# Weight and token parts of a split-precision feed-forward kernel: made by ScalarE and accumulating DMAs instead of VectorE and GpSimd, and six more units computed from parts

## The chip, the cores and the metric

The kernel runs on one core of a Trainium2 chip. The metric is the device time of one execution in microseconds. The kernel before takes 273.64 us (median of three runs, 273.51 to 273.93). One execution was also recorded by the hardware profiler; that one took 273.72 us, of which the profile shows a span of 272.0 us. All times inside the kernel are microseconds from the start of that span.

## The reference

Two blocks follow each other. The first is a linear attention with sketched quadratic features; the second a gated feed-forward block on its output.

```
phi(x)  = outer(S1 x, S2 x)                 # r = 8, so 64 features, per token and head
q_p, k_p = phi(q), phi(k)                   # q, k, v: batch 4, heads 4, 1088 tokens, 32 wide
kv  = sum over s of k_p[s] v[s]             # 64 x 32 per head
z   = sum over s of k_p[s]
x   = (q_p kv) / (q_p z + 1e-6)             # -> 4352 tokens x 128
g   = x @ w_gate ;  val = x @ w_val         # 128 -> 1536
out = (g * sigmoid(g) * val) @ w_out        # 1536 -> 128
```

The inputs come as 64-bit floating-point numbers and are handled as pairs of 32-bit words.

## The kernel before

**Tiles.** Tokens stand in the columns of `xT` (128 features x 4352 tokens) and are worked on in blocks: the first batch's 1088 tokens as blocks 0, 1 and 2 (384, 320 and 384 columns), the rest in blocks of 480. The 1536 hidden features are 12 chunks `j` of 128. A *unit* (i, j) is block i against chunk j: two products into PSUM (gate and value), Silu on ScalarE, the product of both on VectorE into a slot of `hbuf`, `extra`, `soon` or `late`. `down()` multiplies a finished unit by chunk j of `w_out` and sums over j in one PSUM bank for each block.

**Plain units and units of parts.** `unit()` multiplies plain 32-bit floats (line 1043); each of its two products shows as two MATMUL records. The other kind replaces a product by three faster ones in the format fp32r: weight and token are each split into a high part, a low part and a difference part (`w1`, `wb`, `wd` and `x1`, `x0`, `xd`). `start_unit()` (line 1007) makes `wd` times `xd` for gate and value, and ScalarE then scales those sums in PSUM (line 1010). `finish_unit()` adds `w1` times `x1` and `wb` times `x0` for both (lines 1019 and 1020), then Silu (1022) and the product (1027). Both multiply six times in all.

**Where parts come from.** Before they are split, the weights arrive as 64-bit words in pieces, and `narrow()` turns each piece to 32 bits in four steps: VectorE (265, 266), ScalarE (270, 271), VectorE (273, 279), and a multiply on GpSimd (288) that writes the weight. `cut_weights(w, c)` then splits the three chunks 3c to 3c+2 of `w_gate` or `w_val` in four steps, each 128 x 384: `w1` on ScalarE (859), the remainder on GpSimd or VectorE (862), `wb` on ScalarE (864), `wd` on VectorE or GpSimd (867, 871). `cut_tokens(i)` splits a block of tokens, `cut_down()` the chunks 1 to 11 of `w_out`.

**Order.** The schedule is written out by hand: each engine runs its instructions strictly in the order in which the program issues them, and SyncE (SP), ScalarE and GpSimd issue DMAs from the same in-order queues. The stretch that matters here has four stages:

- A list `seq` of 24 units of the first batch, here numbered 0 to 23: (0,3) to (0,5), (2,0) to (2,2), (1,3) to (1,5), (2,3) to (2,5), (0,6) to (0,8), (1,6) to (1,8), (0,9) to (0,11), (1,9) to (1,11). All 24 are plain. From unit 17 on each is followed by a `down()`. Between them `parts[z]` holds the narrowing steps of the last weight pieces and of `w_out`, and `attentions()` gives steps of the next batch's attention through `parts_of()`.
- A loop of ND = 13 `down()` calls with attention steps between: after the eighth come `key_values` (393), `key_products` (359) and `value_sums` (718), which needs the sums that GpSimd makes in `feature_sums` (552); after the eleventh come `query_sketches` (347). The twelfth pass begins with `start_unit(2, 6)`, the first unit of parts.
- Units (2, 6) to (2, 11), of parts, each with a `down()`, then further `down()` calls.
- The main loop over the blocks of 480, all of parts, with the second batch's attention and onward between.

`steps_at` says after which unit or pass of a loop a step of `cut_weights` or `cut_tokens` is issued; the names are `g0` to `g3` and `v0` to `v3` for the four thirds of `w_gate` and `w_val`, `x` for the tokens of block 2. `accum_op` DMAs (issued on GpSimd, which add what they bring to what is there) are already used in the main loop, for the difference part of the hidden values (988), after a plain copy issued on SP (978).

Of the kernel before, what the change touches and what calls it, by code (L numbers as in the profile page):

```python
# [19 lines left out]
def kernel(  # L20
# [599 lines left out]
    def attentions():  # L620
# [4 lines left out]
        kp = pair("keys")  # L625
        for i, c in enumerate(kpieces):
            key_products(kp[:, i, :], *c)
        ka = apool.tile([P, NC * H, R], FP32, tag="kas", name="kas")

        def sketch(ps, i):  # L630
            c0, c1 = kpieces[i]
            return ps[:, i, 0 : 64 * (c1 - c0)].rearrange("p (x t r) -> p x t r", t=2, r=R)

        for i, (c0, c1) in enumerate(kpieces):
            nc.scalar.copy(ka[:, H * c0 : H * c1, :], sketch(kp, i)[:, :, 0, :])
        yield from turn_queries(1)
        phk = apool.tile([P, NC, H, R, R], FP32, tag="phk", name="phk")
        for n, (i, c0, c1) in enumerate(((0, 0, 3), (0, 3, 5), (1, 5, 7), (1, 7, 9))):
            first = H * (c0 - kpieces[i][0])
            kb = sketch(kp, i)[:, first : first + H * (c1 - c0), 1, :]  # L640
            key_features(phk, (ka[:, H * c0 : H * c1, :], kb), c0, c1)
            if n == 0:
                zs, sums = feature_sums(phk)
            else:
                sums.pop(0)()
            if n == 3:
                let_go("keys")
            if n % 3 != 1:
                yield
# [194 lines left out]

    def home(w, c):


# [7 lines left out]
    def cut_weights(w, c, low, engine):  # L855

        w1, wb, wd = w_parts[id(w), c] = home(w, c)
        src = w[:, 3 * c : 3 * c + 3, :]
        nc.scalar.activation(out=w1, in_=src, func=AF.Copy, scale=CUT)
        yield  # L860
        low = low[0]
        engine.tensor_tensor(out=low, in0=src, in1=whole(w1), op=ALU.subtract)
        yield
        nc.scalar.activation(out=wb, in_=low, func=AF.Copy, scale=BETA)
        yield
        if engine is nc.vector:
            nc.vector.scalar_tensor_tensor(
                out=wd, in0=low, scalar=-BETA, in1=whole(w1), op0=ALU.mult, op1=ALU.add
            )
        else:  # L870
            engine.tensor_tensor(out=wd, in0=whole(w1), in1=whole(wb), op=ALU.subtract)

    def cut_tokens(i, engine=nc.gpsimd, soon=False):
# [7 lines left out]
        nc.scalar.activation(x1[:, 0:n], x, AF.Copy, scale=CUT)  # L881

        def low():
            engine.tensor_tensor(
                out=x0[:, 0:n], in0=x, in1=whole(x1[:, 0:n]), op=ALU.subtract
            )

        def difference():
            nc.vector.scalar_tensor_tensor(
                out=xd[:, 0:n], in0=whole(x1[:, 0:n]), scalar=WHOLE, in1=x,  # L890
                op0=ALU.mult, op1=ALU.subtract,
# [33 lines left out]
    def cut_down():  # L925

        n = len(FINE)
        parts = const.tile([P, 3, n, D], F32R, tag="room", name="dparts", bufs=1)
        w1, wb, wd = (parts[:, k] for k in range(3))
        down_parts.update(w1=w1, wb=wb, wd=wd)  # L930

        def high(c):
            nc.scalar.activation(w1[:, c], wo[:, FINE[0] :][:, c], AF.Copy, scale=CUT)

        def left(c):
            nc.gpsimd.tensor_tensor(
                out=wb[:, c], in0=whole(w1[:, c]), in1=wo[:, FINE[0] :][:, c], op=ALU.subtract
            )

        def differ(c):  # L940
            nc.vector.scalar_tensor_tensor(
                out=wd[:, c], in0=whole(wb[:, c]), scalar=BETA, in1=whole(w1[:, c]),
                op0=ALU.mult, op1=ALU.add,
            )

        a, b, c = slice(0, 3), slice(3, 6), slice(6, n)
        high(a)
        yield
        high(b)
        yield  # L950
        high(c)
        add_to(behind, 2, lambda: left(a))
        add_to(behind, 2, lambda: left(b))
        add_to(behind, 5, lambda: differ(a))
        add_to(behind, 6, lambda: differ(b))
        add_to(behind, 2, lambda: left(c))
        add_to(behind, 21, lambda: differ(c))
        yield

# [35 lines left out]
    room = const.tile([P, 10, BW], FP32, tag="room", name="room", bufs=1)  # L995
# [39 lines left out]
    def unit(i, j, late=False, between=(None, None), apart=False):  # L1035
# [10 lines left out]
        sg = room[:, len(lates) + caught[0], :] if late else fpool.tile([P, WB], FP32, tag="sg", name="sg", bufs=5)  # L1046
# [25 lines left out]
    def down(y=None):  # L1072
# [11 lines left out]
        if j in mine:  # L1084
            w1, wb, wd = [down_parts[x][:, FINE.index(j), :] for x in ("w1", "wb", "wd")]
# [22 lines left out]
    def copy_out(y, i, n):  # L1108
# [4 lines left out]
        copy = lambda: nc.scalar.activation(x, p, AF.Copy, scale=-BETA * WHOLE)  # L1113
# [200 lines left out]
    def free(c):  # L1314
        return [room[:, c, :].rearrange("p (c f) -> p c f", f=P)]

# [12 lines left out]

    lows = {}  # L1330
    cuts = {"x": cut_tokens(2, nc.vector, soon=True)}
    for c in (2, 3, 0, 1):
        cuts["g%d" % c] = cut_weights(wg, c, free(8 + c % 2), nc.vector if c else nc.gpsimd)
        lows["v%d" % c] = free(6 + c % 2)
        cuts["v%d" % c] = cut_weights(wv, c, lows["v%d" % c], nc.vector if c == 1 else nc.gpsimd)
# [11 lines left out]
    steps_at = {20: ("v2",), 21: ("v3", "v2", "v3"), 22: ("g2",), 23: ("g3",)}  # L1347
    for z, (i, j) in enumerate(seq):
# [3 lines left out]
        unit(i, j)  # L1352
# [6 lines left out]
        if z >= 17:  # L1359
            next_down()  # L1360
            parts_of(1)
# [132 lines left out]
```

## Time and profile before

| | |
|---|---|
| time, median of three | 273.64 us |
| time of the profiled execution | 273.72 us |
| its span | 272.0 us |
| TensorE (PE) busy | 265.8 us, 98% |
| VectorE (DVE) busy | 223.3 us, 82% |
| ScalarE (ACT) busy | 199.6 us, 73% |
| GpSimd (POOL) busy | 87.5 us, 32% |
| chain that ended last | PE 92% of the span |

Busy shares are means over the whole span. Matmuls are pipelined: a record's duration includes its latency, and the pace is read from the distance between the starts of two neighbours. A row of the timeline holds start, duration, engine, line, operation and tiles, `x2` for two merged instructions; the brackets behind it hold the idle time of the engine before the row, and what ended it. "To landing" is counted from the start of a DMA's issue to its semaphore.

### The profile page before, as it was taken

The page shows a single profiled execution, that of the slowest core. Times are in us where ns is not written, and L with a number is a line of the kernel's source. Part 1 is how long each engine was busy: PE and PEld are TensorE (multiplying, and loading weights), DVE is VectorE, ACT ScalarE, POOL GpSimd, SP SyncE. Part 2 cuts the span into 40 slices and gives each one's busy share as a digit, 9 for nine tenths or more (in the row PEclk, how much of TensorE's full clock was granted, in tenths as well). Part 3 has the DMA queues.
Part 4 walks back from the last instruction along what each step waited for, and adds up shares of the span by engine and source line. Part 5 has one row for each costly group of instructions (what it writes and reads, how often), then busy time and mean ns, then how long its engine had stood idle before and what let it go on. Part 6 is the DMA issues. An engine that isn't in the chain of part 4 may idle for free.

```text
span 272.0 us, 6028 instructions
## 1 busy us (share of the span) xinstructions
PE 265.8 (98%) x2212; PEld 204.0 (75%) x2212; DVE 223.3 (82%) x429; ACT 199.6 (73%) x357; POOL 87.5 (32%) x110
## 2 busy tenths in 40 slices
PE   8899999999999999999999999999999999999994
PEld 7645566666785687886677878867888888889994
DVE  3997988989788798987767889768968996998881
ACT  3468666362686789787579998869989888888870
POOL 3313422249431494470042342223224213222000
PEclk9999999999999999999999999999999999999999
DMA  6573197131331047811137869754476566647221
GB/s 194 172 212 95 49 260 215 40 127 29 94 90 27 1 120 189 180 49 39 39 88 178 177 140 187 180 108 123 86 160 155 118 136 147 146 103 153 39 36 29
DMA packets 36509, 32.01 MB, mean 118 GB/s; under 512 B 20992, under 2 KB 34560, under 8 KB 36480
## 3 DMA queue, kind: packets, MB, share of 16 engines
q1 hardware_dynamic: 30064, 22.13, 28.3%
q0 software_dynamic: 5184, 8.85, 19.0%
q10 hardware_dynamic: 1232, 0.66, 0.9%
q8 instruction: 17, 0.28, 0.4%
q14 instruction: 12, 0.10, 0.1%
HBM read 11.41 MB, written 2.23 MB: 50 GB/s over the span
## 4 chain that ended last, share of the span: by engine, by line
PE 92%; DVE 3%; DMA 2%; ACT 1%; issue 0%; SPq 0%; ACTq 0%
PE PS L1095 14%; PE PS L1019 14%; PE PS L1007 14%; PE PS L1020 14%; PE PS L1043 12%; PE PS L1087 5%; PE PS L1089 5%; PE PS L1090 5%; PE PS L359 2%; PE PS L792 2%; PE PS L347 2%; PE PS L393 2%; DMA kld<-in_k_dram 2%; PE PS L1133 1%; PE PS L502 1%; PE PS L450 1%
## 5 line engine op out<-in xcount | busy, mean ns | idle before, releaser
L1010 ACT ACTIVATE PS<-PS 128x960 f32<-128x960 f32 (+1 forms) x90 | 83.4, 926 | 22.1 <-PE PS L1007 20.6
L1027 DVE SCALAR_TENSOR_TENSOR hbuf<-PS,sg 128x480 f32<-128x480 f32 (+1 forms) x81 | 51.8, 639 | 21.2 <-ACT sg L1022 20.1
L1022 ACT ACTIVATE sg<-PS 128x480 f32<-128x480 f32 (+1 forms) x90 | 49.6, 552 | 2.2 <-PE PS L1020 1.9
L1007 PE MATMUL PS<-xd,wd 128*128 128x480 f32 (+1 forms) x90 | 33.6, 373 | 0.0
L1020 PE MATMUL PS<-x,wb 128*128 128x480 f32 (+1 forms) x90 | 33.5, 372 | 0.0
L1019 PE MATMUL PS<-x,w 128*128 128x480 f32 (+1 forms) x90 | 33.3, 370 | 0.0
L1095 PE MATMUL PS<-hbuf,wo 128*128 128x480 f32 (+3 forms) x80 | 33.0, 505 | 0.0
L1007 PE MATMUL PS<-xd,graw 128*128 128x480 f32 (+1 forms) x69 | 32.6, 472 | 0.0
L1020 PE MATMUL PS<-x,graw 128*128 128x480 f32 (+1 forms) x69 | 25.5, 370 | 0.0
L1043 PE MATMUL PS<-xT,wg 128*128 128x384 f32 (+1 forms) x60 | 23.5, 474 | 0.1
L1043 PE MATMUL PS<-xT,wv 128*128 128x384 f32 (+1 forms) x60 | 23.1, 467 | 0.3 <-DVE wv L288 0.3
L1007 PEld LDWEIGHTS PS<-xd,wd 128*128 128x128 f32 x90 | 16.9, 188 | 6.3 <-issue 2.3
L1047 ACT ACTIVATE sg<-PS 128x384 f32<-128x384 f32 (+1 forms) x24 | 11.2, 468 | 13.2 <-PE PS L1043 12.4
L1019 PEld LDWEIGHTS PS<-x,w 128*128 128x128 f32 x90 | 16.9, 187 | 2.2
L1020 PEld LDWEIGHTS PS<-x,wb 128*128 128x128 f32 x90 | 16.9, 188 | 2.1
L1019 PE MATMUL PS<-x,graw 128*128 128x480 f32 (+1 forms) x48 | 18.0, 376 | 0.0
L1095 PEld LDWEIGHTS PS<-hbuf,wo 128*128 128x128 f32 x80 | 14.8, 189 | 3.8 <-issue 0.4
L1007 PEld LDWEIGHTS PS<-xd,graw 128*128 128x128 f32 x69 | 13.0, 188 | 5.3 <-ACT PS L1010 1.9
L1043 PEld LDWEIGHTS PS<-xT,wv 128*128 128x128 f32 x60 | 11.2, 190 | 7.4 <-DVE hbuf L1058 0.8
L1043 PEld LDWEIGHTS PS<-xT,wg 128*128 128x128 f32 x60 | 10.9, 190 | 7.7 <-issue 1.1
L1019 PE MATMUL PS<-x,gphq 128*128 128x480 f32 (+1 forms) x42 | 16.1, 384 | 0.1
L1020 PEld LDWEIGHTS PS<-x,graw 128*128 128x128 f32 x69 | 13.0, 188 | 1.3
(287 smaller groups left out, 589.5 us busy)
## 6 DMA issues: line engine op xcount, KB each, us to landing
kld<-in_k_dram SPq DMA_DIRECT2D x4, 544.0 KB, 4.2
qld<-in_q_dram SPq DMA_DIRECT2D x3, 544.0 KB, 5.3
raw<-in_moe_w_out_dram SPq DMA_DIRECT2D x4, 384.0 KB, 4.6
hwv<-hwv POOLq DMA_DIRECT2D x6, 240.0 KB, 3.5
hextra<-hextra POOLq DMA_DIRECT2D x6, 240.0 KB, 3.5
vld<-in_v_dram SPq DMA_DIRECT2D x9, 144.0 KB, 5.2
hwv<-hwg SPq DMA_DIRECT2D x5, 240.0 KB, 3.0
hkld<-hqld SPq DMA_DIRECT2D x5, 240.0 KB, 2.5
```

What stands on the lines that cost most here:

```text
L1007: nc.tensor.matmul(ps[:, k], w_parts[id(w), j // 3][2][:, j % 3, :], xd, start=True, stop=True)
L1010: nc.scalar.activation(ps, ps, AF.Copy, scale=-1.0 / WHOLE)
L1019: nc.tensor.matmul(ps[:, k], w1, x1, start=False, stop=False, skip_group_check=True)
L1020: nc.tensor.matmul(ps[:, k], wb, x0, start=False, stop=True, skip_group_check=True)
L1022: nc.scalar.activation(sg, ps[:, 0], AF.Silu, scale=WHOLE)
L1027: nc.vector.scalar_tensor_tensor(out=hj[:, 0:n], in0=ps[:, 1], scalar=WHOLE, in1=sg, op0=ALU.mult, op1=ALU.mult)
L1043: nc.tensor.matmul(o[:, 0:n], w[:, j, :], xT[:, t0 : t0 + n], start=True, stop=True)
L1047: nc.scalar.activation(sg[:, 0:n], g[:, 0:n], AF.Silu)
L1087: nc.tensor.matmul(acc[i][:, 0:n], wd, hd, **sides)
L1089: nc.tensor.matmul(p, w1, h1, start=(j == mine[0]), stop=False)
L1090: nc.tensor.matmul(p, wb, h0, start=False, stop=(j == mine[-1]))
L1095: nc.tensor.matmul(acc[i][:, 0:n], wo[:, j, :], hidden[i, j][:, 0:n], **sides)
```

## The change

`cut_weights` no longer uses VectorE or GpSimd arithmetic. ScalarE makes `w1` with the sign turned; an accumulating DMA issued on GpSimd adds it to the weight in place, which leaves the remainder there, and a DMA issued on SP copies `w1` to `wd`; ScalarE makes `wb` from the remainder; a second accumulating DMA adds `wb` to `wd`. Each of the two accumulating DMAs and the copy moves 128 x 384 floats (192 KB). `cut_tokens` gets the same form of `x0` for blocks 0, 1 and 2 (copy on SP, accumulation on GpSimd), and `cut_down` for its low part, now in four groups of up to three chunks.

The last three chunks (c = 3) of both weights are split right behind their narrowing, during units 10 to 15, and blocks 0 and 1 of the tokens are split as well, so that units 18 to 23 become units of parts. The third with c = 2 and the tokens of block 2 follow in the ND loop; c = 0 and c = 1 later. The keys' sketches of the first `attentions()` step are copied whole from PSUM by ScalarE (both factors, not one). Buffers move: the parts of c = 3 and of `w_out` take over the spots of `room`, now six single tiles, and a new tile `more`.

```diff
-    def cut_weights(w, c, low, engine):
+    def cut_weights(w, c):
         w1, wb, wd = w_parts[id(w), c] = home(w, c)
         src = w[:, 3 * c : 3 * c + 3, :]
-        nc.scalar.activation(out=w1, in_=src, func=AF.Copy, scale=CUT)
+        nc.scalar.activation(out=w1, in_=src, func=AF.Copy, scale=-CUT)
         yield
-        low = low[0]
-        engine.tensor_tensor(out=low, in0=src, in1=whole(w1), op=ALU.subtract)
+        nc.gpsimd.dma_start(out=src, in_=whole(w1), accum_op=ALU.add)
+        nc.sync.dma_start(out=whole(wd), in_=whole(w1))
         yield
-        nc.scalar.activation(out=wb, in_=low, func=AF.Copy, scale=BETA)
+        nc.scalar.activation(out=wb, in_=src, func=AF.Copy, scale=BETA)
         yield
-        if engine is nc.vector:
...
+        nc.gpsimd.dma_start(out=wd, in_=wb, accum_op=ALU.add)
...
     def cut_tokens(i, engine=nc.gpsimd, soon=False):
...
+        if engine is None:
+            nc.sync.dma_start(out=whole(x0[:, 0:n]), in_=x)
         def low():
+            if engine is None:
+                nc.gpsimd.dma_start(out=x0[:, 0:n], in_=x1[:, 0:n], accum_op=ALU.add)
+                return
...
     def cut_down():
...
+            def left(w1=w1, wb=wb):
+                nc.gpsimd.dma_start(out=wb, in_=w1, accum_op=ALU.add)
...
+            nc.scalar.activation(w1, src, AF.Copy, scale=-CUT)
+            nc.sync.dma_start(out=whole(wb), in_=src)
+            add_to(behind, 2, left)
+            add_to(behind, (5, 6, 21, 22)[g], differ)
...
-    steps_at = {20: ("v2",), 21: ("v3", "v2", "v3"), 22: ("g2",), 23: ("g3",)}
+    FIRST = 18
+    steps_at = {
+        10: ("g3",), 11: ("v3", "g3"), 12: ("v3", "x0"), 13: ("g3",), 14: ("v3", "g3", "x0"),
+        15: ("v3", "x1"), 17: ("x1",),
+    }
     for z, (i, j) in enumerate(seq):
...
-        unit(i, j)
+        if z < FIRST:
+            unit(i, j)
+        else:
+            if z + 1 < len(seq):
+                start_unit(*seq[z + 1])
+            finish_unit(i, j)
         for p in parts.get(z, ()):
             part(*p)
...
         if z >= 17:
             next_down()
             parts_of(1)
+        if z + 1 == FIRST:
+            start_unit(*seq[FIRST])
...
     steps_at = {
-        0: ("g2", "v2", "v3"), 1: ("g2",), 2: ("g2", "g3"), 3: ("g3", "v2"), 4: ("g3", "v3"), 5: ("g2",),
-        7: ("x",), 8: ("x", "g3", "v0"), 9: ("g0",),
+        0: ("v2",), 1: ("g2", "v2"), 2: ("g2",), 3: ("x2", "v2"), 4: ("g2",), 5: ("x2", "v2"), 6: ("g2",),
+        8: ("v0",), 9: ("g0", "v0"), 10: ("g0",), 12: ("v0", "g0"),
     }
     ND = 13
...
     steps_at = {
-        7: ("v0", "g0"), 9: ("v0", "g0"), 10: ("v0", "g0"), 11: ("v1", "g1", "v1", "g1"),
+        6: ("v0",), 7: ("g0", "v1"), 8: ("g1", "v1"), 9: ("g1",), 10: ("v1",), 11: ("g1",),
     }
```

The resulting order on GpSimd from unit 10 on is: the narrowing multiply of the last piece of `w_val`; the first accumulations of g3 and v3; the multiply of `w_out` piece 0; the second accumulation of g3; that of the tokens x0; the second accumulation of v3; the multiply of `w_out` piece 1; tokens x1; the multiplies of pieces 2 and 3; the four operations of `feature_sums`; the first accumulations of v2 and g2; the tokens x2; the second accumulations of v2 and g2; then those of c = 0 and c = 1. On ScalarE, `wb` of g3 stands ahead of unit 14's Silu, and `wb` of v3 ahead of unit 15's.

## The prediction

> **What bounds the kernel now.** I read the page's busy shares and the chain that ended last first.
>
> ```profile
> PE 265.8 (98%) x2212; PEld 204.0 (75%) x2212; DVE 223.3 (82%) x429; ACT 199.6 (73%) x357; POOL 87.5 (32%) x110
> ...
> PE 92%; DVE 3%; DMA 2%; ACT 1%; issue 0%; SPq 0%; ACTq 0%
> ```
>
> TensorE is the chain. A busy PE need not be at its peak, so I then read TensorE's own timeline, start to start.
>
> ```profile
> 45.19 0.70 PE L1043 MATMUL PS<-xT,wg 128*128 128x320 f32 x2
> ...
> 48.42 0.81 PE L1095 MATMUL PS<-hbuf,wo 128*128 128x384 f32 x2
> 49.06 0.81 PE L1043 MATMUL PS<-xT,wg 128*128 128x384 f32 x2
> 49.71 0.81 PE L1043 MATMUL PS<-xT,wv 128*128 128x384 f32 x2
> 50.35 0.81 PE L1095 MATMUL PS<-hbuf,wo 128*128 128x384 f32 x2
> ...
> 72.39 0.44 PE L1007 MATMUL PS<-xd,graw 128*128 128x384 f32 x1
> ...
> 74.27 0.34 PE L1019 MATMUL PS<-x,graw 128*128 128x384 f32 x1
> 74.44 0.34 PE L1020 MATMUL PS<-x,graw 128*128 128x384 f32 x1
> ```
>
> Plain products of 384 columns follow each other by 0.645 us, products of parts by 0.174. From about 30 us to 240 us nearly every distance is at its pace: the matmul work itself sets the end, and nothing downstream has slack to take back a TensorE stall. A microsecond of product saved is a microsecond gained, a microsecond waited is one lost. VectorE and GpSimd work taken away gains nothing by itself.
>
> **Part 1: six units of parts (gain).** A plain unit of 384 columns takes 2 x 0.645 = 1.29 us, one of parts 6 x 0.174 = 1.05: 0.245 saved, three times. At 320 columns the plain unit takes 1.075 (45.19 to 46.26), and six parts scaled from 0.174 at 384 and 0.217 at 480 take 6 x 0.146 = 0.88: 0.195 saved, three times. Sum: **-1.3 us**. That is all that TensorE can gain.
>
> **Part 2: the parts of c = 3 come too late.** GpSimd's timeline and the accumulating DMAs that the kernel already has:
>
> ```profile
> 41.87 1.00 POOL L288 TENSOR_TENSOR wv<-man,exp 128x384 f32<-128x384 f32 x1 [1.61 <-DVE man L279]
> 47.03 1.00 POOL L288 TENSOR_TENSOR wo<-man,exp 128x384 f32<-128x384 f32 x1 [4.16 <-DVE man L279]
> ...
> 62.30 1.27 POOL L552 TENSOR_TENSOR zs<-phk 128x512 f32<-128x512 f32 x1
> 63.65 2.81 POOL L552 TENSOR_TENSOR zs<-zs,phk 128x512 f32<-128x512 f32 x2
> 66.54 0.93 POOL L552 TENSOR_TENSOR zs<-zs 128x256 f32<-128x256 f32 x1
> 67.55 0.94 POOL L552 TENSOR_TENSOR zs<-zs,phk 128x256 f32<-128x256 f32 x1
> ```
>
> ```profile
> L988 POOL DMA_DIRECT2D hwv<-hwv x6: 862/862/877, 105.6 to 238.9; - x6
> ...
> DMA to landing us min/median/max: 3.1/3.3/5.1
> ```
>
> An accumulation occupies GpSimd for 0.86 us and lands 3.1 us after its issue began (240 KB; these move 192 KB, so I take the least of the 38). GpSimd is in order: the first accumulation of g3 stands behind the multiply of w_val's last piece, so it starts at 42.9 and lands at 46.0; v3's follows at 43.8 and lands at 46.9. ScalarE is in order too:
>
> ```profile
> 44.76 0.48 ACT L1047 ACTIVATE sg<-PS 128x384 f32<-128x384 f32 x1
> ...
> 46.05 0.43 ACT L1047 ACTIVATE sg<-PS 128x320 f32<-128x320 f32 x1
> ```
>
> `wb` of g3 now stands ahead of unit 14's Silu (44.76) and waits until 46.0. With 0.5 us for it, that Silu ends at 46.9 and VectorE's product at 47.5. Before, v3's `w1` waits for the same w_val multiply (42.9) and holds units 12 and 13 by about a microsecond. `wb` of v3 (to 48.2) then holds unit 15's Silu to 48.6. The four PSUM banks give two units of lead, so unit 16's gate waits until 46.95 (was 46.26), unit 17's until 48.6 (was 47.34), and unit 17's value product, which reuses the bank of unit 16's gate, until 49.4 behind one more ScalarE step. Unit 17 ends at 49.95 instead of 48.42: **+1.5 us**.
>
> Next, w_out's piece 0: its VectorE steps follow unit 14's product, end at 48.4, and GpSimd multiplies until 49.45 (was 48.03). Only behind that, in order, it issues g3's second accumulation (49.45), the tokens' (50.3) and v3's (51.15, landing 54.25). TensorE has done unit 17 and one `down` by 50.6 and then needs both `wd`. It would have started the second `wd` product at 50.77: **+3.5 us**. The scaling of unit 18's sums (0.80 us, as at 73.04 on ScalarE, with about 0.2 of latency) has only unit 19's 0.35 us of products over it: **+0.7 us**.
>
> This does not hang on my reckoning of ScalarE. With no hold at all the multiply still ends at 48.03 as it did, two more issues of 0.86 make 49.75, plus 3.1 makes 52.85, against 49.23: 3.6 us.
>
> **Part 3: the same again at c = 2.** Call T0 the start of the ND loop: 61.43 before; 4.4 later by the steps above, 65.8. In the new order the first accumulations of v2 and g2 stand behind the four `feature_sums` operations, 6.2 us in the rows at 62.30 to 68.49. These wait for VectorE's features, which follow the products of units 22 and 23; I get them from T0 + 1.4 to T0 + 7.6. `value_sums`, at T0 + 7.3, waits **+0.3 us**. Then, in order: v2 and g2 issue, g2 from T0 + 8.5, landing at T0 + 11.6; `wb` 0.5; g2's second accumulation issues at T0 + 12.15 and lands at T0 + 15.3. TensorE arrives at unit (2, 6) at T0 + 11.3 (72.39 is T0 + 10.96 in the trace, plus the 0.3): **+4.0 us**. The cover before was that parts of c = 2 were ready without a round trip; `wd` of g2 was written by 68.9, 3.5 us ahead.
>
> **Edits at nothing.** c = 0 and c = 1: two DMA trips plus `wb` are under 8 us, and their readers start some 15 us later. `cut_down`: four issues of 0.86 follow the second `feature_sums`, as 3.50 us of multiplies did (97.94), and land by about 104.7, where the first reader on VectorE stands at 104.77; if that cover is gone, it costs what is missing, up to 1 us. Sketch copies twice as wide cost ScalarE about 0.4 us and hide in unit 20's 1.5. SP's copies wait only for `w1` and land within 2.2 to 4.3 us (lines of 978), ahead of the second accumulations; the loads behind them are needed 10 us later.
>
> **A rule beside the row.** The landing row is 3.1 us. The Trainium skill, "DMA: Bandwidth & Descriptors", section "Anatomy of one DMA — SWDGE (gpsimd) path", fits about 2.0 us plus bytes over 436e3 for each such DMA: 2.45 us for 192 KB. By it the three trips on the way would each be 0.65 shorter and the sum about 2 us lower. The same skill, "TensorE: Matmul & The Clock Gate", section "Part 1: The HAM clock gate", halves the clock after an idle window of about 3.4 us, which speaks against this change: each of the two long waits could add an estimated 1.7 us. The granted clock is full in every row of this trace, and no gap in it is long enough to show it.
>
> **The sum.** -1.3 + 1.5 + 3.5 + 0.7 + 0.3 + 4.0 = +8.7 us. The profiled execution took 273.72, so 282.4; the median lies 0.08 lower: **282.3 us**.
>
> **The rivals.** *The late parts cost only once* (0.13): if `feature_sums` runs earlier or the c = 2 trips are short, part 3 vanishes, and 282.3 - 4.3 = 278.0. For: VectorE has less to do there. Against: the sums wait for the features, which wait for TensorE, so both shift together. *Faster* (0.09, of it 0.02 no more than within 0.2%): one mechanism, the accumulations landing before unit 18 because GpSimd would issue them without queueing behind piece 0's multiply. Then only part 1 is left, 273.6 - 1.3 = 272.3. For: the steps are two to three units apart in the program, 2.6 to 3.9 us, about one trip. Against: the multiply's row at 47.03 and the strict order; it decides at a total wait of 1.3 us, and the floor of part 2 is 3.6. *Longer trips* (0.14): around 43 us the DMA engines also load w_out and the queries (4.6 and 5.3 us to landing). If trips take 4.5 us instead of 3.1, the first `wb` slips by 1.4, the last landing before unit 18 by 1.4, and two trips of part 3 likewise: up to 5.6 more; half of it gives 285. My forecast has 0.64.
>
> **Range.** Low end of the terms: part 2 without hold at 3.6 + 0.7, part 3 with sums at the unloaded pace of rows like 47.03 (384 columns in 1.0 us, so 0.9 less in all) 3.1, no other wait: +6.1, or 279.8; it must reach the first rival: 278. High: longer trips at 285, and somewhat beyond: 286.5. About 0.2 us is what this measurement can tell from no change; faster 0.07, same 0.02, slower 0.91.
>
> **What would show it.** On TensorE: idle of 3 to 4 us before unit 18's difference products, released by an accumulating DMA, and about 4 us before unit (2, 6); part units of 1.05 and 0.88 us between; the rest at the old pace. On ScalarE: waits of 0.5 us or more before `wb` of g3. On GpSimd: second accumulations queued behind the w_out multiply and behind `feature_sums`. I am wrong if unit 18 starts by 50 us, if the accumulations land within 1 us, or if a later stage gets the time back.

## The result, and the profile after

The changed kernel takes **297.98 us** (median of six, 296.52 to 299.67), the kernel before 273.71 in as many runs beside it: a ratio of 1.088, 95% interval 1.084 to 1.092. It is 24 us slower where I forecast 8.7. The profiled execution took 296.52, with a span of 294.8.

The page of the changed kernel: busy shares, the granted clock in 40 slices, two rows of the DMA queues, and the chain that ended last.

```profile
PE 273.4 (93%) x2224; PEld 208.3 (71%) x2224; DVE 220.9 (75%) x423; ACT 204.3 (69%) x366; POOL 96.4 (33%) x122
...
PEclk9999999769995999999999999999999999999999
...
q1 hardware_dynamic: 32224, 24.98, 29.1%
q0 software_dynamic: 8496, 13.27, 26.9%
...
PE 78%; DMA 6%; DVE 5%; issue 4%; POOL 2%; SPq 2%; ACT 2%; DVEq 0%; POOLq 0%; ACTq 0%
```

TensorE was 92% of the chain and is 78%; DMA (2% before) and VectorE (3%) have grown in it, GpSimd and SP's queue have entered it. VectorE's busy share fell from 82% to 75%, but mostly because the span is longer: its busy time fell only from 223.3 to 220.9 us. The clock row drops in two places. Here is who made TensorE wait (total, times, longest):

```profile
PE PS L1000 <- DMA graw<-graw: 7.8, 1, 7.8
PE PS L1036 <- ACT sg L1040: 2.8, 2, 2.4
PE PS L1000 <- DMA more<-more: 2.0, 1, 2.0
...
PE PS L1012 <- ACT PS L1003: 0.5, 1, 0.5
```

The plain product (L1036) waits for a Silu: that is the hold ahead of units 16 and 17. The difference products (L1000) wait for the parts of units 18 and (2, 6), L1012 for the scaling. These are the four waits that the forecast named, in their places; three differ much in size (2.8, 2.0 and 7.8 us where 1.5, 3.5 and 4.0 were forecast). TensorE's timeline shows them. L1012 and L1013 are the other products of a part unit, L1088 is the `down` product:

```profile
49.31 0.81 PE L1036 MATMUL PS<-xT,wg 128*128 128x320 f32 x2 [2.41 <-ACT sg L1040]
...
53.41 1.36 PE L1088 MATMUL PS<-hbuf,wo 128*128 128x384 f32 x2
54.90 0.44 PE L1000 MATMUL PS<-xd,more 128*128 128x384 f32 x1
57.29 0.81 PE L1000 MATMUL PS<-xd,more 128*128 128x384 f32 x3 [1.95 <-DMA more<-more]
...
59.42 0.52 PE L1012 MATMUL PS<-x,wroom 128*128 128x384 f32 x1
59.74 0.52 PE L1013 MATMUL PS<-x,more 128*128 128x384 f32 x1
...
92.27 0.66 PE L1000 MATMUL PS<-xd,graw 128*128 128x384 f32 x1 [7.83 <-DMA graw<-graw]
```

Unit 16's gate product stood at 46.26 before, and starts at 49.31 (+3.05); the `down` at 48.42 starts at 53.41 (+5.0); unit (2, 6) at 72.39 starts at 92.27 (+19.9). The two rows at 59 us are 0.32 apart where products of parts had been 0.174 apart: the clock. Three windows of the changed kernel; the last three columns are granted clock, DMA share and GB/s:

```profile
40.00:45.00 5.00, 5.00 (x17) 2.82 (x16) 2.94 (x7) 3.08 (x8) 3.32 (x4) 1.00 1.07 297
57.00:65.00 8.00, 7.20 (x27) 5.17 (x29) 3.14 (x8) 4.09 (x7) 0.00 (x0) 0.57 0.34 88
92.00:96.00 4.00, 3.73 (x10) 2.98 (x11) 0.05 (x1) 1.65 (x3) 0.00 (x0) 0.57 1.04 248
```

The clock is at half from 51.1 to 54.5, 57.9 to 64.8 and 88.6 to 95.5 us, after waits of TensorE of 2.4 and 2.0 us, and from within the one of 7.8 us that began at 84.4.

Who was late? First ScalarE, then GpSimd, at the two places:

```profile
48.36 0.52 ACT L858 ACTIVATE more<-wg 128x384 fp32r<-128x384 f32 x1 [2.45 <-DMA wg<-wroom]
...
86.00 0.52 ACT L858 ACTIVATE wb<-wv 128x384 fp32r<-128x384 f32 x1 [13.10 <-DMA wv<-w]
87.17 0.52 ACT L858 ACTIVATE graw<-wg 128x384 fp32r<-128x384 f32 x1 [0.65 <-DMA wg<-graw]
```

```profile
43.00 1.00 POOL L855 DMA_DIRECT2D wg<-wroom  x1
43.92 1.01 POOL L855 DMA_DIRECT2D wv<-wroom  x1
50.87 1.00 POOL L288 TENSOR_TENSOR wo<-man,exp 128x384 f32<-128x384 f32 x1 [5.94 <-DVE man L279]
51.83 0.85 POOL L860 DMA_DIRECT2D more<-more  x1
52.41 1.16 POOL L876 DMA_DIRECT2D x<-x  x1
52.95 1.51 POOL L860 DMA_DIRECT2D more<-more  x1
...
79.61 0.72 POOL L552 TENSOR_TENSOR zs<-zs,phk 128x256 f32<-128x256 f32 x1
80.28 0.88 POOL L855 DMA_DIRECT2D wv<-w  x1
80.88 1.17 POOL L855 DMA_DIRECT2D wg<-graw  x1
...
87.99 0.85 POOL L860 DMA_DIRECT2D graw<-graw  x1 [0.32 <-DMA spread<-spread]
```

The order is the forecast one: first accumulation (L855), `wb` on ScalarE (L858), second accumulation (L860), the latter behind piece 0's multiply. A trip is the time from the start of the issue to the landing. The trips on the path are longer: g3's first accumulation is issued at 43.00, and ScalarE gets it at 48.3: 5.3 us. v3's second goes from 52.95 to TensorE's start at 57.29 (4.3), g2's first from 80.88 to ScalarE's start at 87.17 (6.3), g2's second from 87.99 to 92.27 (4.3). I had put 3.1 for each. An accumulation with nothing ahead of it does take that: g3's second is issued at 51.83, and TensorE's first difference product of unit 18 starts at 54.90, 3.1 us later. What follows it on the queue lands later; queue q0 (GpSimd's DMAs) and two landings, between 53 and 58 us of the changed kernel:

```profile
q0 software_dynamic: 576, 0.75, 96.6%
...
x<-x POOLq DMA_DIRECT2D x1, 192.0 KB, 3.7
more<-more POOLq DMA_DIRECT2D x1, 192.0 KB, 4.3
```

In these 5 us q0 is the only queue that moves anything, and its 0.75 MB (151 GB/s) keep the 16 DMA engines busy for 96.6% of the time.

### The profile page after: what moved, and what is told of

The parts are those of the page before. It is cut to its first block, busy times and chain, and to the rows that moved or that the text cites. A ratio compares the mean times of both kernels' runs of the same rounds, so it can differ in the third digit from the quotient of the medians.

```text
span 294.8 us, 6132 instructions
## 1 busy us (share of the span) xinstructions
PE 273.4 (93%) x2224; PEld 208.3 (71%) x2224; DVE 220.9 (75%) x423; ACT 204.3 (69%) x366; POOL 96.4 (33%) x122
## 3 DMA queue, kind: packets, MB, share of 16 engines
q1 hardware_dynamic: 32224, 24.98, 29.1%
q0 software_dynamic: 8496, 13.27, 26.9%
## 4 chain that ended last, share of the span: by engine, by line
PE 78%; DMA 6%; DVE 5%; issue 4%; POOL 2%; SPq 2%; ACT 2%; DVEq 0%; POOLq 0%; ACTq 0%
PE PS L1000 13%; PE PS L1012 13%; PE PS L1013 13%; PE PS L1088 12%; PE PS L1036 6%; PE PS L1080 4%; PE PS L1083 4%; PE PS L1082 4%; PE PS L780 2%; PE PS L359 2%; PE PS L393 2%; DMA kld<-in_k_dram 1%; DMA more<-more 1%; DMA graw<-graw 1%; SPq L1150 1%
## 5 line engine op out<-in xcount | busy, mean ns | idle before, releaser
L1003 ACT ACTIVATE PS<-PS 128x960 f32<-128x960 f32 (+2 forms) x96 | 87.8, 915 | 31.4 <-PE PS L1000 29.7
L1020 DVE SCALAR_TENSOR_TENSOR hbuf<-PS,sg 128x480 f32<-128x480 f32 (+2 forms) x84 | 53.3, 634 | 26.0 <-ACT sg L1015 24.6
L1015 ACT ACTIVATE sg<-PS 128x480 f32<-128x480 f32 (+2 forms) x96 | 52.5, 546 | 3.9 <-PE PS L1013 3.7
L1088 PE MATMUL PS<-hbuf,wo 128*128 128x480 f32 (+3 forms) x80 | 36.0, 545 | 0.0
L1000 PE MATMUL PS<-xd,graw 128*128 128x480 f32 (+1 forms) x45 | 22.4, 497 | 7.8 <-DMA graw<-graw 7.8
L1000 PE MATMUL PS<-xd,wd 128*128 128x480 f32 (+1 forms) x66 | 24.9, 378 | 0.0
L1013 PE MATMUL PS<-x,wb 128*128 128x480 f32 (+1 forms) x66 | 24.6, 372 | 0.0
L1012 PE MATMUL PS<-x,w 128*128 128x480 f32 (+1 forms) x66 | 24.5, 371 | 0.0
L1012 PE MATMUL PS<-x,wroom 128*128 128x480 f32 (+2 forms) x60 | 23.1, 386 | 0.5 <-ACT PS L1003 0.5
L1036 PE MATMUL PS<-xT,wg 128*128 128x384 f32 (+1 forms) x48 | 19.8, 495 | 2.9 <-ACT sg L1040 2.8
L1000 PE MATMUL PS<-xd,more 128*128 128x480 f32 (+2 forms) x60 | 20.5, 424 | 2.1 <-DMA more<-more 2.0
L1013 PE MATMUL PS<-x,more 128*128 128x480 f32 (+2 forms) x60 | 22.3, 372 | 0.0
L1036 PE MATMUL PS<-xT,wv 128*128 128x384 f32 (+1 forms) x48 | 19.3, 486 | 0.3 <-DVE wv L288 0.3
L1088 PEld LDWEIGHTS PS<-hbuf,wo 128*128 128x128 f32 x80 | 16.1, 207 | 3.1 <-issue 1.2
L1013 PE MATMUL PS<-x,graw 128*128 128x480 f32 (+1 forms) x45 | 16.7, 370 | 0.7 <-issue 0.7
L1000 PEld LDWEIGHTS PS<-xd,graw 128*128 128x128 f32 x45 | 8.7, 194 | 11.8 <-issue 9.1
L1000 PEld LDWEIGHTS PS<-xd,more 128*128 128x128 f32 x60 | 11.2, 193 | 7.4 <-DMA more<-more 3.4
L1000 PEld LDWEIGHTS PS<-xd,wd 128*128 128x128 f32 x66 | 12.7, 193 | 5.1 <-issue 1.7
L1012 PE MATMUL PS<-x,gphq 128*128 128x480 f32 (+1 forms) x42 | 16.1, 383 | 0.1
L1036 PEld LDWEIGHTS PS<-xT,wg 128*128 128x128 f32 x48 | 8.7, 194 | 10.0 <-ACT sg L1040 4.2
L1012 PEld LDWEIGHTS PS<-x,w 128*128 128x128 f32 x66 | 12.4, 188 | 2.5 <-issue 0.9
L1036 PEld LDWEIGHTS PS<-xT,wv 128*128 128x128 f32 x48 | 9.0, 196 | 6.8 <-DVE soon L1051 1.1
```

Source lines behind the costliest of these rows:

```text
L1000: nc.tensor.matmul(ps[:, k], w_parts[id(w), j // 3][2][:, j % 3, :], xd, start=True, stop=True)
L1003: nc.scalar.activation(ps, ps, AF.Copy, scale=-1.0 / WHOLE)
L1012: nc.tensor.matmul(ps[:, k], w1, x1, start=False, stop=False, skip_group_check=True)
L1013: nc.tensor.matmul(ps[:, k], wb, x0, start=False, stop=True, skip_group_check=True)
L1015: nc.scalar.activation(sg, ps[:, 0], AF.Silu, scale=WHOLE)
L1020: nc.vector.scalar_tensor_tensor(out=hj[:, 0:n], in0=ps[:, 1], scalar=WHOLE, in1=sg, op0=ALU.mult, op1=ALU.mult)
```

## The experiments

Parts are named by chunk group: the fourth is c = 3 (units 18 to 23), the third c = 2 (unit (2, 6) on), the first two c = 0 and 1. The kernel before, run beside them, took 273.8 to 274.1 us (medians).

**1. TensorE kept busy in the three waits.** What is the half clock worth?

```diff
+        if z in (16, 17):
+            keep_warm({16: 9, 17: 3}[z], ps=PS[:, 5, :])
...
+            keep_warm(17, ps=PS[:, 5, :])      # ahead of start_unit of unit 18
+            keep_warm(30, ps=PS[:, 3, :])      # ahead of start_unit(2, 6)
```

> The changed kernel with products nobody reads put into TensorE's three waits (9 ahead of unit 16, 3 ahead of unit 17, 17 ahead of the first difference products of unit 18, 30 ahead of unit (2, 6); 0.216 us each at full clock, 512 columns), which should end before the parts land. Theory 'the waits also halve the clock': the profile of the changed kernel shows three stretches at half clock, 17.1 us in all, in which TensorE worked about 13 us; with the clock kept up the time falls by about 6 us, from 298 to 292, and the granted clock is 1.0 throughout. Rival 'only the waits count, the next stage takes the half clock back': it stays at 297 to 298, since the same parts land at the same times.

294.37 us (293.71 to 295.15), ratio 1.074 (1.071 to 1.078). The clock row of this kernel's page:

```profile
PEclk9999999999999999999999999999999999999999
```

The clock is full, and the time is **3.6 us** less, where I expected more. In the profiled run the parts of unit 18 came even later: g3's first trip took 5.9 us (42.82 to 48.70), v3's second 5.0 (53.27 to 58.26), so the product behind them starts 1.0 us later than in the changed kernel, which is lost from the gain. Between the two profiled executions the gain is 2.4 us.

This edit touches no DMA, so the longer trips are scatter: in the eight profiled executions whose DMAs up to there are those of the changed kernel (the changed kernel and experiments 1 to 5, 8 and 12), g3's first trip took 5.3 to 6.6 us.

**2. The six units plain again**, all DMAs kept.

```diff
-    FIRST = 18
+    FIRST = 24
```

> The changed kernel with units 18 to 23 plain again; all steps of the parts stay where they are. Theory 'the parts of c = 3 land too late for unit 18': TensorE's offset against the kernel before is 11.3 us at the end of unit 18 in the changed kernel; the wait for the two difference parts, the scaling and the half clock after it go, the hold of ScalarE ahead of units 16 and 17 (3 to 5 us) stays: 298 falls by 5 to 7, to 291 to 293. Rival 'the hold on ScalarE is the whole of it': less than 2 us less, since the hold is still there.

291.10 us (289.27 to 291.81), ratio 1.060 (1.056 to 1.065): 7 us less. The hold of units 15 to 17 stays (3.3 us for `sg`), as does the wait before unit (2, 6) (7.9), and the wait before unit 18 is gone.

**3. The third chunks and block 2 on VectorE**, the rest as changed.

For c = 2 alone (`engine` is VectorE there), in place of the DMAs:

```diff
-        nc.gpsimd.dma_start(out=src, in_=whole(w1), accum_op=ALU.add)
-        nc.sync.dma_start(out=whole(wd), in_=whole(w1))
...
+            engine.tensor_tensor(out=src, in0=src, in1=whole(w1), op=ALU.add)
...
-        nc.gpsimd.dma_start(out=wd, in_=wb, accum_op=ALU.add)
...
+            engine.tensor_tensor(out=wd, in0=whole(w1), in1=whole(wb), op=ALU.add)
```

> The changed kernel with the remainder and the difference of c = 2 of both weights and the low part of block 2's tokens made by VectorE again, at the same places in the order; the rest as changed. Theory 'two trips behind the feature sums are the second wait': the 7.8 us before unit (2, 6) and the half clock after it (1.5 us) go, and VectorE has the room (it waits 7.9 us there): 298 falls by 8 to 9.5, to 288.5 to 290. Rival 'the second wait is a follow-up of the first, something else is then late there': less than 4 us less.

297.45 us (296.67 to 299.16), ratio 1.086 (1.082 to 1.091): **a miss**, nothing gained. Unit (2, 6) starts at 85.16, 7.1 us earlier, and TensorE then waits in a new place. Rows of this kernel from TensorE, VectorE, ScalarE and GpSimd (L780 is the numerators, L1026 the product of a part unit, L861 a `wb`, L864 a second accumulation):

```profile
104.01 2.56 PE L780 MATMUL PS<-phT,spread 32*32 32x288 f32 x64 [5.84 <-DVE phT L762]
...
102.51 0.56 DVE L1026 SCALAR_TENSOR_TENSOR soon<-PS,sg 128x384 f32<-128x384 f32 x1 [6.15 <-ACT sg L1021]
...
101.58 0.52 ACT L861 ACTIVATE wb<-wv 128x384 fp32r<-128x384 f32 x1 [6.80 <-DMA wv<-w]
...
94.94 0.85 POOL L864 DMA_DIRECT2D wd<-wb  x1 [11.48 <-DMA gphq<-gphq]
```

Read from the top: the numerators wait for VectorE's `phT`; VectorE had waited for a Silu; the Silu stood behind the `wb` of the second value chunk; that accumulation, which took 5.5 us to land, stood on GpSimd (issued at 96.01) behind one ahead of which GpSimd sat idle for 11.5 us, at the end for a copy on SP. That copy was issued at 91.94, behind the stores (81.34), the moves of `spread` (84.09, 5.1 us of issues) and a load (89.27). What I had costed at nothing had been hidden by the stall in front of it.

**4. Both of the last two.** 

> Units 18 to 23 plain and c = 2 on VectorE, together. Theory 'two places, each with its own price': the gains of the two runs before add up, 298 falls by 13 to 16.5, to 281.5 to 285, and what is left against 273.7 is the hold ahead of units 16 and 17, 3 to 5 us with its half clock, and a rest of 1.5 us in later stages, plus 1.3 us of part units not made. Rival 'the accumulating DMAs slow everything': it stays above 287.

289.03 us (287.30 to 290.19), ratio 1.054 (1.049 to 1.059). A miss by 4 us for the same reason: the wait for `phT` is 5.8 us here too.

**5. All DMAs out but those of the fourth chunks, the tokens of blocks 0 and 1, and w_out** (first chunks on GpSimd, the others on VectorE, same edit).

> The changed kernel with c = 2 and c = 1 on VectorE and c = 0 on GpSimd (remainder and difference), and block 2's low part on VectorE; only c = 3, the tokens of blocks 0 and 1 and w_out keep the DMAs. The run with c = 2 alone gained 7.1 us at unit (2, 6) and lost it 20 us later: TensorE waited 5.8 us for VectorE, which waited for a Silu on ScalarE behind `wb` of v1, which waited 6.8 us for its accumulation, which stood on GpSimd behind that of v0, which waited 11.5 us for a plain copy on SP. Theory 'one chain through the in-order queues of GpSimd and SP, whose end shows wherever its cover ends': 298 falls by 9 to 11, to 287 to 289. Rival 'VectorE's order is what holds the numerators': it stays at 297.

289.51 us (median of three, 288.99 to 291.69; the profiled execution took 293.35), ratio 1.059 (1.054 to 1.063), 8.5 us less than the changed kernel and just outside the expected 287 to 289. The wait for `phT` is gone; one of 2.5 us for `s` is new. With the third experiment: the third chunks' and the first two chunks' chains cost 8.5 us together, whichever of them TensorE meets first.

**6. The fourth chunks and those tokens on VectorE as well**; only w_out's parts are made by DMAs.

> As the run before, and c = 3 and the tokens of blocks 0 and 1 on VectorE as well: the six units stay units of parts, and only w_out's parts keep the DMAs. Theory 'the DMA trips are the whole loss, the six units a gain of 1.3': 272.5 to 274, if VectorE, 85% busy at 40 to 60 us before, takes 2.8 us more there. Rival 'VectorE becomes the bound there': 275 to 278, with TensorE waiting for it between 45 and 55 us.

283.90 us (281.50 to 284.62), ratio 1.033 (1.029 to 1.037): 5.6 less, but 6 us above the higher of the two expectations, a miss. The six runs fall into two groups by the mean granted clock: 281.5 and 281.6 us at 1.0, 283.8 to 284.6 at 0.993 to 0.994. The longest wait of TensorE, and VectorE's rows ahead of it:

```profile
PE PS L347 <- DVE s L613: 2.5, 1, 2.5
```

```profile
44.86 0.54 DVE L859 TENSOR_TENSOR wv<-wv,wroom 128x384 f32<-128x384 f32 x1
...
68.12 1.63 DVE L859 TENSOR_TENSOR wv<-wv,w 128x384 f32<-128x384 f32 x1
69.68 1.08 DVE L859 TENSOR_TENSOR wg<-wg,graw 128x384 f32<-128x384 f32 x1
...
72.62 1.35 DVE L866 TENSOR_TENSOR wd<-w,wb 128x384 fp32r<-128x384 f32 x1
73.89 1.34 DVE L866 TENSOR_TENSOR graw<-graw 128x384 fp32r<-128x384 f32 x1
```

L859 makes a remainder, L866 a difference part. My own arrangement put six operations ahead of the small ones that make `s`, and four of them take 1.1 to 1.6 us where the form of L859 took 0.54 at 44.86 in the same run. GpSimd runs beside all four: its feature sums until 71.3 us, then two additions of its own (72.4 to 74.8). In this execution the clock is at half from 75.7 to 79.1 us, from the end of that wait on.

**7. The fourth chunks' and tokens' plain copies by VectorE instead of SP**, accumulations kept.

```diff
-        nc.sync.dma_start(out=whole(wd), in_=whole(w1))
+        if c == 3:
+            nc.vector.tensor_copy(wd, whole(w1))
+        else:
+            nc.sync.dma_start(out=whole(wd), in_=whole(w1))
...
+            if i < 2:
+                nc.vector.tensor_copy(x0[:, 0:n], x)
```

> The changed kernel with the four plain copies of c = 3 and of the tokens of blocks 0 and 1 made by VectorE (which idles there) and not by DMAs from SP: 720 KB less to move between 42 and 48 us. Theory 'trips take 5.3 us there because the DMA engines are full': the first accumulation of g3 lands in 3.5 to 4.5 us, TensorE's wait before unit 16 falls from 2.4 to about 1, the time by 1 to 3. Rival 'an accumulation takes 5 us by itself': 5.3 us again.

One run, 297.29 us. g3's first accumulation now lands 4.8 us after issue instead of 5.3, and the wait of unit 16 falls to 1.3 us; TensorE then waits longer for `more` (3.8 in place of 2.0), and starts the second difference product of unit 18 at 56.70 instead of 57.29.

**8. Piece 0 of w_out multiplied on VectorE**, so that the second accumulations do not queue behind it.

> The changed kernel with the narrowing multiply of w_out's piece 0 on VectorE and not on GpSimd, so that the second accumulations of c = 3 no longer stand behind it. Theory 'the queue behind the multiply is the main part of the wait before unit 18': g3's second accumulation issues at about 49.0 instead of 51.8, v3's at about 50.8 instead of 53, the last lands by 54.5 instead of 57.3: 2 to 4 us less. Rival 'they wait for ScalarE's `wb` anyway': less than 1 us.

One run, 294.36 us: 2 to 5 less than the changed kernel's runs. The wait for `more` falls from 2.0 us to 0.4, while the hold (2.4) and the wait before unit (2, 6) (8.2) stay. In this execution TensorE was 1.9 us late from its first plain unit on (17.22 instead of 15.36), after a stretch at half clock from 7.6 to 11.0 us that the changed kernel's profile does not have. Unit (2, 6) still starts 3.0 us earlier (89.32), so the place in the queue was worth more than the two times show.

**9. The second batch's loads left out** (35 to 38 us on SP), to empty the DMA engines around 43 us.

```diff
-            load_k(1)
-            load_v(1, [nc.sync] * 4)
-            load_q(1)
```

> The changed kernel without the second batch's loads of keys, values and queries that SP issues at 35 to 38 us (the first batch's data stay in their tiles, so the second batch's outputs are computed from them). Theory 'loaded engines': the first accumulations landed 5.3 us after their issue at 43 us, where I had put 3.1, because the 16 DMA engines were full (share 1.03 between 40 and 50 us); with some 1.6 MB less ahead of them they land 3.1 to 4.0 us after issue, the wait of unit 16 for Silu falls from 2.4 us to under 1.0, and the time falls by 1.5 to 3.5 us, to 294.5 to 296.5. Rival 'the trip itself': an accumulating DMA of 192 KB takes 5 us beside its twin from the same queue; landing and wait stay within 0.5 us of the changed kernel's and the time within 1 us of 298.

297.65 us (297.29 to 298.98), ratio 1.087 (1.084 to 1.089): no change. The same window and the first `wb` of this kernel:

```profile
40.00:45.00 5.00, 5.00 (x17) 2.84 (x16) 2.84 (x7) 3.08 (x8) 3.38 (x4) 1.00 0.56 176
```

```profile
47.61 0.52 ACT L858 ACTIVATE more<-wg 128x384 fp32r<-128x384 f32 x1 [1.60 <-DMA wg<-wroom]
```

With the DMA share at 0.56 instead of 1.07, the trip (issued at 43.09) is 4.5 us. Against the changed kernel's profile the loads made up 0.8 of the 2.2 us that I had missed; against the scatter of 5.3 to 6.6 us, 0.8 at the least. And the time doesn't move, because TensorE starts the second difference product of unit 18 at 56.55, only 0.7 earlier: most of what it saves in the hold it waits for `more`, and later waits are longer (8.9 before unit (2, 6)).

**10. The kernel of experiment 6, with w_out's low parts added on GpSimd** instead of copied by SP and accumulated.

```diff
-                nc.gpsimd.dma_start(out=wb, in_=w1, accum_op=ALU.add)
+                nc.gpsimd.tensor_tensor(out=wb, in0=src, in1=whole(w1), op=ALU.add)
...
-            nc.sync.dma_start(out=whole(wb), in_=src)
```

> The kernel with all remainders and differences of gate, value and token parts on engines (283.9 us), and now the low parts of w_out by four 128x384 additions on GpSimd in place of SP's copies and accumulating DMAs: no accumulating DMA is left but those of the hidden units, which the kernel before has too. Theory 'the w_out DMAs push the hidden units' DMAs back on GpSimd's queue': the waits for hwg and hwv (0.6 and 0.5 us) and the later steps go, 1.5 to 3 us less, 281 to 282.4. Rival 'the drift is the fourth piece and the order of VectorE's work': within 0.6 us of 283.9.

282.49 us (281.66 to 284.29), ratio 1.031 (1.027 to 1.035). The intervals overlap, and no gain is shown: the two runs at a clock of 0.999 and 1.0 took 281.7 us, as the two of experiment 6 at full clock did (281.5 and 281.6), so the medians differ by the mix of clocks. The waits for `hwg` and `hwv` are gone, others for `hkT`, `hqld` and `hextra` (0.6, 0.5 and 0.3 us) stand in their place; TensorE's lag against the kernel before (its `down` products, start against start) ends at 9.6 us instead of 10.6.

**11. And the third chunks back in the places and on the engines of the kernel before.**

```diff
-        cuts["v%d" % c] = cut_weights(wv, c, nc.vector if c else nc.gpsimd)
+        cuts["v%d" % c] = cut_weights(wv, c, nc.gpsimd if c == 2 else (nc.vector if c else nc.gpsimd))
...
-        15: ("v3", "x1"), 17: ("x1",),
+        15: ("v3", "x1"), 17: ("x1",), 20: ("v2",), 21: ("v2",), 22: ("g2",),
...
-        0: ("v2",), 1: ("g2", "v2"), 2: ("g2",), 3: ("x2", "v2"), 4: ("g2",), 5: ("x2", "v2"), 6: ("g2",),
...
+        0: ("g2",), 1: ("g2",), 2: ("v2",), 3: ("v2",), 5: ("g2",), 7: ("x2",),
```

> The last one, with the splitting of the third chunks put back to where and on what engine the kernel before has it (value part's two operations on GpSimd ahead of the feature sums, gate part's on VectorE ahead of the fold, tokens of block 2 behind it). What is left of the change is the six units made of parts early, with the three chunks split at units 10 to 15, and the order of first and second chunks. Theory 'VectorE's own queue held the fold': the wait before the feature products of the second batch (2.5 us for the tile s) and the slow half-clock stretch after it go; 3.5 to 6 us less than the last one, 275.5 to 278. Rival 'the six units are worth their 1.3 us': 272.5 to 274, faster than or equal to the kernel before. Rival 'the hold of units 15 to 17 keeps the rest late': within 2 us of the last one.

280.00 us (279.06 to 281.18), ratio 1.022 (1.020 to 1.024): 2.5 us less than experiment 10, and 1.7 less than that experiment's runs at full clock: less gained than expected, though the wait for `s` is gone and the clock is full. TensorE's longest waits in this kernel (L1093 is the plain `down` product, L1085 the one of parts):

```profile
PE PS L1093 <- POOL wo L288: 1.4, 2, 1.2
PE PS L1085 <- DMA hextra<-hextra: 1.0, 1, 1.0
```

**12. The changed kernel, with only the third chunks' DMAs issued earlier** (high parts and first accumulations at units 20 to 22, ahead of the feature sums).

> The changed kernel with only the third chunks' copies and accumulations moved ahead: high parts and first accumulations at units 20 to 22, ahead of GpSimd's feature sums, second accumulations one or two steps earlier; still all DMAs. Theory 'lead would have covered the trips': the wait before unit (2,6) falls from 7.8 us to under 2, but the chains of the first two chunks and the Silu behind them take part of it back as they did when these chunks went to VectorE; 292 to 296. Rival 'lead is enough': 290 to 292. Rival 'all of it is taken back later': within 1 us of 298.

300.89 us (300.29 to 303.79), ratio 1.100 (1.096 to 1.104): **slower still**, outside all three expectations. TensorE's waits in this kernel:

```profile
PE PS L780 <- DVE phT L762: 3.8, 1, 3.8
PE PS L1036 <- ACT sg L1040: 3.7, 1, 3.7
PE PS L347 <- DVE s L613: 2.6, 1, 2.6
```

The 7.8 us before unit (2, 6) are gone, and the start of that unit is 4.2 us earlier (88.06); but `s` and then `phT` are late, the latter as in experiment 3, and at the numerators nothing is left of it. The hold is 3.7 us here: g3's first trip took 6.6 us in this execution, ahead of everything that this experiment moves, and TensorE was 1.6 us later at the first `down` than in the changed kernel's profile. So part of the 2.9 us between the medians may be that scatter.

**13. The kernel of experiment 11 with the six units plain**, the fourth chunks split where the kernel before does.

> The kernel with engines for all low parts and the third chunks in their old places (280.0 us), and now units 18 to 23 plain again and the fourth chunks split where the kernel before splits them (units 21 to 23 and the steps behind them). What it tells is what the six units of parts are worth by themselves, with no DMA in them. Theory 'the hold eats the gain': their work on ScalarE and VectorE keeps units 15 to 17 back by up to 2.8 us, and the last multiply of w_out behind them, against 1.3 us of shorter products; without the six units 1.5 to 3.5 us less, 276.5 to 278.5. Rival 'the hold is made up later': within 0.7 us of 280.0. Rival 'they gain': 0.7 us or more above 280.0.

276.52 us (276.02 to 276.78), ratio 1.009 (1.006 to 1.012). No accumulating DMA but the old ones on either side, and the six units of parts, with the early splitting that they need, *cost* 3.5 us. (v3's two operations are back on GpSimd here as well, as in the kernel before.)

**14. The kernel of experiment 11 with the first two chunks where the kernel before has them.**

> The same kernel of 280.0 us with only the steps of the first and second chunks put back to the places that the kernel before has; the six units stay as parts. Theory 'their order costs the step of 0.7 us near 136 us and the late accumulations of hidden units behind it': 0.7 to 2.5 us less, 277.5 to 279.3. Rival: within 0.6 us of 280.0; what is left of the difference then comes from the six units or from the fourth piece of w_out.

279.62 us (278.56 to 280.37), ratio 1.020 (1.016 to 1.024): the rival, no difference that shows.

## Why the prediction was wrong

The direction was right, and the time lies 11.5 us above my range. As a ladder from the runs, each step one more part of the change undone:

| kernel | us | step |
|---|---|---|
| changed | 298.0 | |
| first three chunks and block 2 without DMAs (5) | 289.5 | -8.5 |
| fourth chunks and blocks 0, 1 without DMAs (6) | 283.9 | -5.6 |
| w_out without DMAs (10) | 282.5 | -1.4, not shown: none at equal clock |
| third chunks in their old places (11) | 280.0 | -2.5 |
| the six units plain (13) | 276.5 | -3.5 |
| before | 273.8 | -2.7 |

The first two steps, which take the accumulating DMAs of the weights and tokens out of the way, are 14 of the 24 us. Point by point, in the profiled execution, whose span grew by 22.8 against my 8.7. TensorE's lag against the kernel before was 5.0 us at the first `down` (I had 1.5), 10.5 at the start of the ND loop (4.4), 19.9 at unit (2, 6) and 22.8 at the end (8.7 for both):

**The term that was mis-sized: an accumulation's trip, 3.1 us.** I took it from the hidden units' rows, as the least of 38 whose largest is 5.1 in the line that I showed. The four trips on the path took 5.3, 4.3, 6.3 and 4.3 us, 7.8 us more in all. My rival "longer trips" had the loads as their cause and 4.5 us as their length.

For the 4.3 before unit 18 the trace shows why. Three accumulations are issued at 51.83, 52.41 and 52.95; they land 3.0, 3.7 and 4.3 us after their issue, that is about 1.2 us behind each other, while no other queue moves anything. The whole run has the same pace: queue q0, which carries GpSimd's accumulating DMAs and nothing else, moves 13.27 MB in 26.9% of the 16 engines' 294.8 us, that is 167 GB/s for all of them, or 1.2 us for 192 KB; q1, SP's, 24.98 MB in 29.1%, 291 GB/s. The kernel before had 8.85 MB at 19.0%, 171 GB/s: this could have been read beforehand.

For the two first accumulations (5.3 and 6.3) it isn't settled. g3's has none of its kind ahead of it; between 41 and 50 us q1 takes 77.8% of the engines and q0 24.9%. Without the second batch's loads it took 4.5 us (experiment 9), without SP's copies 4.8 (experiment 7), each one execution and both below the scatter of 5.3 to 6.6; no run leaves out both.

**The hold, +1.5, became +5.0 at the `down`.** Unit 16 starts 3.05 late because `wb` of g3 begins at 48.36, where I had 46.0: 2.2 us of trip. Of the other 1.9 us, 0.7 is unit 17's gate, which starts late behind a Silu as well (0.41 us idle), and 1.2 the half clock from 51.1 on.

**The wait before unit 18.** I had it end at 54.25; it ended at 57.29, 3.0 later. The multiply starts at 50.87, not 48.45 (+2.4: its narrowing steps on ScalarE had queued behind the `wb` that waited); the trip is 1.2 longer; the issues stand closer than I had them (1.1 us instead of 1.7). That GpSimd's order sets this point, as I had argued, is shown by experiment 8 (without the multiply the wait is 0.4 us). Experiments 7 and 9 agree: a landing of the first accumulation 0.6 to 0.8 us earlier moved the end of the wait by 0.6 to 0.7, while the hold fell by 0.9 to 1.1. That the wait itself is 2.0 us and not 3.5 is the hold: TensorE came later.

**The clock, in no term.** I had it in a sentence of its own, as an estimate of 1.7 us for each of two waits. The three half-clock stretches of 3.4, 6.8 and 6.8 us cost 3.6 us by experiment 1, somewhat more if its later landing is counted. That my two times 1.7 come near this is luck: they stood for two stretches of 3.4 us, and there were 17 us at half clock, in part of which TensorE waited anyway. The Trainium skill, "TensorE: Matmul & The Clock Gate", section "Part 1: The HAM clock gate", from which I had worked them out, gives a window of about 3.4 us of idleness; that is longer than the waits of 2.4 and 2.0 us after which the clock fell here, and the measurement decides.

**Part 3, +4.3, became 9.4 at the start of unit (2, 6)** (TensorE's lag was 10.5 at the loop's start, and 19.9 there). In it the wait is 7.8 instead of 4.0; 1.2 us more had gathered in the loop ahead of it (the last multiply of w_out 0.5, `zs` 0.4). GpSimd's sums end where I had them against the loop's start, within a microsecond. g2's two trips were 3.2 and 1.2 longer. Behind that start TensorE worked at half clock, another 1.5 us. The fit of the Trainium skill, "DMA: Bandwidth & Descriptors", section "Anatomy of one DMA — SWDGE (gpsimd) path", which gives an estimated 2.45 us for this size, is further off than my row; the measured 4.3 to 6.3 decide.

**"Edits at nothing" failed twice.** The first two chunks: their cover was the stall ahead of them, and as soon as that is gone they stall TensorE by 5.8 us (experiment 3). SP's copies "wait only for `w1`": they wait for everything that SP issues ahead of them; in that run GpSimd's queue stood for 11.5 us until one had landed. For w_out, whose DMAs I had land in time, no cost is shown: the ladder's 1.4 us go with the clock of the runs.

**Part 1, -1.3, has the wrong sign as a whole.** The products are shorter, as reckoned: in experiment 11 TensorE's lag falls from 2.8 to 1.6 us over the six units. But splitting their weights earlier puts ScalarE and VectorE work in front of units 15 to 17 (2.8 us of lag), holds w_out's last multiply (1.2 us of wait), and, which I had not thought of, the main loop then loses 2.4 to 3.7 us more in experiments 6, 10 and 11, where TensorE waits for hidden parts (in 11 `hextra` and `hkT`), while with six plain units it loses at most 0.5 (experiments 2 and 13). The pattern isn't clean: it loses 1.7 us with six plain units in experiment 4, and only 1.4 with six of parts in the changed kernel. Why six units of parts should make those late isn't settled. Nor is the last 2.7 us, which stand as three waits of 0.6 to 0.9 us (for `zs`, `hbuf` and `phT`) in experiment 13; that kernel still has the wider copies of the sketches, w_out's parts in four groups, the moved buffers and the new order of the first two chunks.

What was right: four waits in their places, their releasers, and that no later stage gives the time back.

## What to carry to other kernels

A trip's duration is a property of its neighbourhood: take it from rows where as many such DMAs stand beside each other as the change will put there, or divide the queue's bytes by the time that its packets took. Before an edit is costed at nothing, ask what would hide it if the stall ahead of it were taken away, since a stall covers whatever is late behind it. Work that moves off a busy engine gains nothing while another engine sets the end, and each DMA between two engines' steps puts its trip, and the queues on both sides of it, into an in-order chain.

## What was not expected of the hardware

Accumulating DMAs from GpSimd moved 167 GB/s for the share of the 16 engines that their packets took, SP's plain ones 291. Three that were issued within 1.1 us, with the engines otherwise free, landed after 3.0, 3.7 and 4.3 us. TensorE's clock fell to half after waits of 2.4 and 2.0 us and stayed there for 3.4 and 6.8 us, through work. Four of VectorE's additions of two 128x384 operands took 1.1 to 1.6 us beside GpSimd's sums and additions, where one took 0.54 with GpSimd idle (44.86, experiment 6). It isn't always VectorE that pays: two at 48.20 and 48.67 took 0.54 beside a multiply on GpSimd, which took 1.72 instead of 1.0.
